# Top-k attention and max-out layers on one core: the GpSimd product of scores and signs in two halves, with a new order of work

## The chip, the cores and the metric

The kernel runs on one core of one Trainium2 chip. The metric is device time in microseconds (us) of one execution. The core has five engines with a queue each: TensorE (PE: matmuls, with their weight loads in a row of their own, PEld), VectorE (DVE), ScalarE (ACT), GpSimd (POOL) and SyncE (SP), which issues the transfers.

## What is computed

Attention with a top-k mask over 8 batches of 8 heads, 576 tokens, head size 64, and then a layer with the maximum of three products, for the 4608 tokens:

```python
def _attn_ref(q, k, v):
    top_k = 32
    scores = matmul(q, k.transpose(0, 1, 3, 2)) / sqrt(D)
    kth = np.partition(scores, -top_k, axis=-1)[..., -top_k:-top_k + 1]
    scores = np.where(scores >= kth, scores, -1000000000.0)
    attn = np.exp(scores - np.max(scores, axis=-1, keepdims=True))
    attn = attn / (np.sum(attn, axis=-1, keepdims=True) + 1e-09)
    return np.matmul(attn, v)

def _moe_ref(x, w1, w2, w3, w_out):
    h = np.maximum(np.maximum(x @ w1, x @ w2), x @ w3)
    return h @ w_out
```

d_model is 512, d_ff 768; everything is float32.

## The kernel before

**Attention** runs in 144 units. A unit is 128 query rows of a pair of heads (or the last 64 rows of two pairs), so it has two score tiles of 128 x 576. Its steps, with their keys in the order's table: scores on PE (`q`, L508) and their copy out of PSUM on ACT (`e`, L516); the top eight of each of 7 column groups on DVE (`s0`, `s1`, L525); from these a pivot close to the 32nd largest (`N` on POOL, L531; `p1` to `p5` on DVE, L539 to L557, of which `p4`, L554, reads two tiles of SBUF). Then for each of the two score tiles: the sign of score against pivot on ACT with a count (`g`, L564), the product of scores and signs on POOL (`w`, L569, function `window`), and the top eight of that product on DVE (`k`, L573, `below`), which gives the candidates next to the pivot. Small steps on POOL (`i`, `j`, L580 to L586) and DVE (`h`, L591) pick the 32nd largest. The mask on DVE (`m`, L614, a `scalar_tensor_tensor` that reads the scores twice) follows, then the exponential on ACT (`x`, L623), the denominator (POOL L629, DVE L633, ACT L638), transposes on PE (`T`, L664 to L669) with copies on ACT (`E`, L681), and for a group of units the product with v (`v`, L700), scaled on DVE (`y`, L710) and split into two float16 parts (`Y` on ACT L724, `Z` on POOL L728).

**Weights** come in at the start and are decoded on DVE (L254 to L260), scaled and cut into float16 halves (L272 to L334); `wi_scaled` is the list of the three steps that give the scales of w1, w2 and w3.

**The layers** (`mlp`) run for each batch in two or three pieces of its columns: 36 matmuls for each of six blocks of d_ff (L757), their maximum on ACT and DVE (L764, L766), two parts of h (ACT L769, POOL L772), the second layer (L817), a scaled copy (L822) and the store. A piece can start when the attention of its columns is done. The layers fill PE between attention's steps; the last batch's stand at the end.

**The order** of the instructions of every engine is made ahead by `in_order`: a greedy planner with a cost for each step, a rank (the unit's number plus an entry of `OFFSETS` by step) and waiting times between engines (`GAP`, `NEAR`, `LATE`). `SWITCH` is the price of changing PE's mode (scores use halves of its rows, the product with v halves of its columns); `STICK` says how much later a step may start to keep PE in such a mode; `PATIENCE` how much later than the earliest one a step of better rank may start; `LEAD` how far ranks may run ahead. Steps marked `alone` (p4, the masks, the decoding) are planned with POOL's queue in mind (`LOCK_A`, `LOCK_B`). The engines then run their queues in that order and wait for each other by semaphores.

Of the kernel before, what the change touches and what calls it, by code (L numbers as in the profile page):

```python
# [14 lines left out]
ALU = mybir.AluOpType  # L15
# [9 lines left out]
NSSB = 5  # L25
NWB = 6
PMB = 2
GAP = 67.0
NEAR = 182.0
SWITCH = 100.0  # L30
STICK = 204.0
WINDOW = 150
LEAD = 49.1
LOCK_A = -150.0
LOCK_B = -100.0
OFFSETS = {'E0': -2.08, 'E1': -11.9, 'E2': 1.81, 'N': -19.09, 'T0': 7.0, 'T1': 7.99, 'T2': 7.02, 'Y': -1.5, 'Z': -8.28, 'd':
# [9 lines left out]
RANK_M = -20.0  # L46
LATE = {'PE': 160.0, 'DVE': 85.0, 'ACT': 100.0, 'POOL': 40.0, 'SP': 2000.0}

# [1 line left out]
class Piece:  # L50
# [7 lines left out]
    def seen(self, engine):  # L58

        if engine == self.engine:  # L60
            return self.start + self.cost + (NEAR if engine in ("DVE", "ACT") else 0.0)
        return self.start + self.cost + LATE[self.engine] + GAP

# [6 lines left out]
def in_order(pieces, fill):  # L70
# [35 lines left out]
    while left:  # L106
        best = None
        low = min((q[0].rank for q in queues.values() if q), default=0.0)
        for e in LATE:
            some = [x for x in queues[e][:WINDOW] if x.rank <= low + LEAD]  # L110
            some = some + fills[e][:1] if e == "PE" else fills[e][:1] + some
            could = [(t, x) for x in some if (t := ready(x)) is not None]
            if could:
                first = min(t for t, _ in could)
                stays = [c for c in could if c[1].mode and c[0] <= first + STICK] if e == "PE" and mode[0] else []
                t, x = stays[0] if stays else next(c for c in could if c[0] <= first + PATIENCE[e])
                if best is None or t < best[0]:
# [13 lines left out]
        left -= 1  # L131


PATIENCE = {'PE': 162, 'DVE': 131, 'ACT': 0, 'POOL': 85, 'SP': 0}


@with_exitstack
def kernel(ctx, tc, q, k, v, moe_w1, moe_w2, moe_w3, moe_w_out, out):
    nc = tc.nc
    B, NP, _, S = q.shape  # L140
    D = v.shape[-1]
    P = 128
    C = S // 64
    NU = S // P
    DM, DF = moe_w1.shape
    DO = moe_w_out.shape[1]
    KC = DM // P
    FC = DF // P
    HALF = S // 2
# [61 lines left out]
    CUTS = {DF: DF // 2, DO: DO}  # L211
# [131 lines left out]
    def piece(engine, cost, run, needs=(), rank=0.0, takes=(), mode=None, alone=False, tag=""):  # L343
        x = Piece(engine, cost, run, needs, rank + OFFSETS.get(tag, 0.0), [(rings[r], rel) for r, rel in takes], mode, alone)
        pieces.append(x)
        return x
# [9 lines left out]
    lows = {}  # L356
# [47 lines left out]
    wo_scaled, wi_scaled = [], []  # L404
# [161 lines left out]
    def window(n, t):  # L566

        d = st[n]
        nc.gpsimd.tensor_tensor(d["w"][t], d["ssb"][t], d["w"][t], ALU.mult)  # L569

    def below(n, t):
        d = st[n]
# [161 lines left out]
    def mlp(b, first, spans, tiles, alone, needs, rank):  # L734
# [6 lines left out]
        def add(engine, cost, run, needs=(), takes=(), mode=None):  # L741
            x = Piece(engine, cost, run, needs, rank, [(rings[r], rel) for r, rel in takes], mode)
            every.append(x)
            if engine == "PE":
                if products:
                    x.needs.append(products[-1])
                products.append(x)
            return x

        def layer(i, f, kcs, c0, c1, box):  # L750
            xh, xl = x_of[b]
            if kcs[0] == 0:
                box["ps", i] = ps_m.tile([P, 512], F32, name="m")
            for kc in kcs:
                high, low = halves(i, kc, f * P, P)
                for k, (a, bb) in enumerate(((high, xh), (low, xh), (high, xl))):
                    nc.tensor.matmul(box["ps", i][:, :c1 - c0], a, bb[:, kc, c0:c1], start=(kc == 0 and k == 0),  # L757
                                     stop=(kc == KC - 1 and k == 2))

        def largest(i, w, box):  # L760
            ps, prev = box.pop(("ps", i)), box.get("h")
            h1 = box["h"] = wk.tile([P, WIDE], F32, name="h1", bufs=3)
            if i == 0:
                nc.scalar.activation(h1[:, :w], ps[:, :w], AF.Copy, scale=rises[:, 0:1])  # L764
            else:
                nc.vector.scalar_tensor_tensor(h1[:, :w], ps[:, :w], rises[:, i:i + 1], prev[:, :w], ALU.mult, ALU.max)  # L766

        def high_h(f, cs, w, box):
            nc.scalar.copy(H[0][:, f, cs], box["h"][:, :w])  # L769

        def low_h(f, cs, w, box):
            nc.gpsimd.tensor_tensor(H[1][:, f, cs], box["h"][:, :w], H[0][:, f, cs], ALU.subtract)  # L772

        for c0, c1 in spans:
            w = c1 - c0
            base = min(c0, 2 * P)
            cs = slice(off + c0 - base, off + c1 - base)
            for f in range(FC):
                box, prev, before = {}, None, []
                for i in range(3):  # L780
                    rel = []
                    for kcs in ((0, 1), (2, 3)):
                        x = add("PE", 6 * max(0.434 * w, 64.0), lambda i=i, f=f, kcs=kcs, c0=c0, c1=c1, box=box: layer(i, f, kcs, c0, c1, box),
                                [*needs, *(lows[i * KC + kc, f * P // CUTS[DF] * CUTS[DF]] for kc in range(KC) if lows)],
                                [("m", rel)] if kcs[0] == 0 else [])
                    now = []
                    y = add("DVE" if i else "ACT", 85 + 1.2 * w if i else 125 + 0.97 * w, lambda i=i, w=w, box=box: largest(i, w, box),
                            [x, *prev] if i else [x, *wi_scaled], [("h1", now)])
                    rel.append(y)
                    if i:  # L790
                        before.append(y)
                    before, prev = now, [y]
                y = add("ACT", 87 + 0.85 * w, lambda f=f, cs=cs, w=w, box=box: high_h(f, cs, w, box), prev)
                z = add("POOL", 2.7 * w, lambda f=f, cs=cs, w=w, box=box: low_h(f, cs, w, box), [y])
                before.extend([y, z])
                done.setdefault(f, []).append(z)
# [22 lines left out]
        def scaled_out(n, both, box):  # L819
            so = so_of["both", b] if both else so_of[b]  # L820
            box["ob"] = io.tile([P, DO], F32, name="ob")
            nc.scalar.activation(box["ob"][:n], box["po"][:n], AF.Copy, scale=so[:n])  # L822
# [11 lines left out]
        for u in tiles:  # L834
# [10 lines left out]
            y = add("ACT", 575, lambda n=n, both=both, box=box: scaled_out(n, both, box), [x, so_at[b]], [("ob", used)])  # L845
# [19 lines left out]
    def group_us(b, u):  # L865

        for g in ((0,), (1, 2), (3,)) if b == 0 else ((0, 1), (2, 3)):
            if u in g:
                return g
        return (u,)  # L870
# [14 lines left out]
    def attention(n):  # L885
# [34 lines left out]
        for t in range(2):  # L920
            p(("g", t), "ACT", 770, lambda t=t: sign(n, t), needs=[d["p5"], d["e"]])
            p(("w", t), "POOL", 1410, lambda t=t: window(n, t), needs=[d["g", t]])
            p(("k", t), "DVE", 668, lambda t=t: below(n, t), needs=[d["w", t]])
            held(n, "w", t).append(d["k", t])
# [121 lines left out]
    for b in range(B):  # L1046
        for first, spans, tiles in parts_of[b]:
            us = [u for u in range(NU + 1) if any(c0 < u * P + 64 <= c1 or c0 < (u + 1) * P <= c1 for c0, c1 in spans)]
            needs = [z for (hp, u), z in z_of[b].items() if set(group_us(b, u)) & set(us)]
            products, every, last = mlp(b, first, spans, tiles, False, needs, RANK_M)  # L1050
            fill.extend(every)
        x_done[b].append(last)
# [20 lines left out]
    with tc.If(redo != 0):  # L1073
        with tc.For_i(0, B, 1) as b:
# [6 lines left out]
            for hp in range(NP):  # L1081
# [5 lines left out]
                for u in (*range(NU), *((NU,) if hp % 2 else ())):  # L1087
                    i = len(units)
# [17 lines left out]
            for first, c0, c1, tiles in ((True, 0, 2 * P, (0, 1)), (False, 2 * P, S, range(2, NU + 1))):  # L1106
                for x in mlp(B, first, [(c0, c1)], tiles, True, [], 0.0)[1]:
                    x.run()
# [46 lines left out]
```

## Time and profile before

| | |
|---|---|
| median of 3 runs | 1251.83 us (1251.45 to 1253.36) |
| profiled execution | 1251.33 us, its span 1249.5 us |
| busy, PE / DVE / ACT / POOL | 93% / 91% / 83% / 69% of the span |
| mean granted TensorE clock | 0.976 of full speed |

Busy shares are over the whole span; the views by stretch tell more, since at the start the weights come in and at the end PE is alone. Matmuls are pipelined and their ends are modelled, so PE's busy time is a little more than its work. A line such as L569 is that of the kernel's text, an arrow in a row stands between what is written and what is read, and a bracket at the end of a timeline row holds the idle time before it and what ended it.

### The profile page before, as it was taken

The numbers are of one execution on the slowest core, as the hardware profiler recorded it, in microseconds if no ns is written. First come the engines' busy times: TensorE is split into PE (matmuls) and PEld (weight loads), VectorE is DVE, ScalarE is ACT, GpSimd is POOL, SyncE is SP. The second block draws the span as 40 slices with busy tenths as digits, with TensorE's granted clock in tenths as the row PEclk, the third lists the DMA queues.
The fourth block names the chain that finished last, engine by engine and source line by source line (L and its number), as shares of the span: only waits on it lengthen the run. The fifth ranks groups of instructions, "written<-read, shape, count | busy, mean of one in ns | idle before, by whom it ended". The sixth has DMA issues, their size and how long they took to land.

```text
span 1249.5 us, 30550 instructions
## 1 busy us (share of the span) xinstructions
PE 1158.7 (93%) x9891; PEld 839.8 (67%) x9891; DVE 1141.2 (91%) x5547; ACT 1036.4 (83%) x2406; POOL 866.0 (69%) x1293
## 2 busy tenths in 40 slices
PE   4677789998999999999999999999899999999997
PEld 2355568775776757676777768666676768776764
DVE  8999898999999999999999999999999999999511
ACT  3688899898789998899889998898888988998621
POOL 5456687876677787777787778767777777877410
PEclk9788899999899999999999999999899999999999
DMA  8440111100111011100111021101011010000000
GB/s 329 130 139 1 56 40 48 39 28 23 36 40 47 11 55 28 58 11 20 47 48 39 11 64 40 37 11 39 29 39 47 11 47 19 13 7 2 18 18 29
DMA packets 33864, 54.74 MB, mean 44 GB/s; under 512 B 12960, under 2 KB 12960, under 8 KB 33696
## 3 DMA queue, kind: packets, MB, share of 16 engines
q1 hardware_dynamic: 33696, 52.71, 13.5%
q8 instruction: 80, 1.31, 0.4%
q14 instruction: 88, 0.72, 0.2%
HBM read 43.25 MB, written 9.44 MB: 42 GB/s over the span
## 4 chain that ended last, share of the span: by engine, by line
PE 61%; DVE 27%; ACT 8%; issue 2%; POOL 1%; DMA 0%; ACTq 0%; DVEq 0%; POOLq 0%
PE m L757 26%; PE tr L700 9%; PE s L508 9%; PE tr L669 7%; DVE L L525 7%; PE m L817 6%; DVE ssb L614 5%; DVE Q L573 4%; ACT pm L623 2%; ACT w L564 2%; PE tr L664 2%; DVE h L766 1%; DVE z L554 1%; ACT ssb L516 1%; ACT pT L681 1%
## 5 line engine op out<-in xcount | busy, mean ns | idle before, releaser
L569 POOL TENSOR_TENSOR w<-ssb,w 128x576 f32<-128x576 f32 x288 | 432.0, 1506 | 62.0 <-ACT w L564 58.8
L757 PE MATMUL m<-xh,wall 128*128 128x256 f16 (+3 forms) x2448 | 438.4, 279 | 5.8 <-DVE h L766 3.2
L757 PEld LDWEIGHTS <-wall 128*128 128x128 f16 x3672 | 347.3, 98 | 82.5 <-issue 13.5
L757 PE MATMUL m<-xl,wall 128*128 128x256 f16 (+3 forms) x1224 | 339.0, 279 | 0.0
L525 DVE MAX8 L<-ssb 128x8 f32<-128x82 f32 (+1 forms) x2016 | 316.7, 228 | 2.2 <-ACT ssb L516 2.1
L623 ACT ACTIVATE pm<-ssb,nb 128x576 f32<-128x576 f32 x288 | 224.1, 780 | 49.6 <-DVE ssb L614 49.3
L614 DVE SCALAR_TENSOR_TENSOR ssb<-ssb,kth 128x576 f32<-128x576 f32 x288 | 257.6, 910 | 0.1
L681 ACT COPY pT<-tr 128x512 f32<-128x512 f32 (+1 forms) x432 | 217.7, 514 | 28.3 <-PE tr L666 17.9
L564 ACT ACTIVATE w<-ssb,Q 128x576 f32<-128x576 f32 x288 | 223.4, 778 | 15.7 <-DVE Q L557 14.1
L573 DVE MAX8 Q<-w 128x8 f32<-128x576 f32 x288 | 214.3, 748 | 3.7 <-POOL w L569 3.4
L669 PE MATMUL tr<-ident,pm 128*128 128x128 f32 x1152 | 179.7, 282 | 24.0 <-ACT pm L623 14.3
L508 PE MATMUL s<-kT,qT 64*128 64x288 f32 x1920 | 176.5, 320 | 19.2 <-ACT ssb L516 8.7
L700 PE MATMUL tr<-pT,vt 128*64 128x256 f32 (+2 forms) x2000 | 180.8, 331 | 2.2 <-ACT s L195 1.1
L508 PEld LDWEIGHTS s<-kT,qT 64*128 64x128 f32 x1920 | 139.6, 194 | 62.6 <-ACT ssb L516 22.5
L669 PEld LDWEIGHTS tr<-ident,pm 128*128 128x128 f32 x1152 | 131.1, 142 | 69.2 <-ACT pm L623 29.9
L516 ACT ACTIVATE ssb<-s 128x1152 f32<-128x1152 f32 x144 | 163.2, 1134 | 11.4 <-PE s L508 10.7
L700 PEld LDWEIGHTS tr<-pT,vt 128*64 128x64 f32 x2000 | 112.3, 140 | 63.1 <-issue 20.8
L766 DVE SCALAR_TENSOR_TENSOR h<-m,rises,h 128x256 f32<-128x256 f32 (+3 forms) x204 | 100.2, 491 | 53.6 <-PE m L757 51.4
L772 POOL TENSOR_TENSOR hl<-h,hh 128x256 f16<-128x256 f32 (+3 forms) x102 | 82.8, 811 | 74.8 <-ACT hh L769 73.1
L817 PE MATMUL m<-wall,hh 128*128 128x512 f16 x432 | 128.5, 379 | 0.1
L629 POOL TENSOR_SCALAR den<-sums 128x2 f32<-128x2 f32 x144 | 39.4, 273 | 83.1 <-ACT pm L623 73.5
L817 PE MATMUL m<-wall,hl 128*128 128x512 f16 x216 | 81.9, 379 | 0.0
(116 smaller groups left out, 1505.8 us busy)
## 6 DMA issues: line engine op xcount, KB each, us to landing
raw<-in_k_dram SPq DMA_DIRECT2D x36, 288.0 KB, 2.8
raw<-in_q_dram SPq DMA_DIRECT2D x36, 256.0 KB, 2.8
vt<-in_v_dram SPq DMA_DIRECT2D x32, 256.0 KB, 2.8
out_dram<-ob SPq DMA_DIRECT2D x32, 256.0 KB, 2.0
wall<-in_moe_w_dram SPq DMA_DIRECT2D x8, 768.0 KB, 6.5
wall<-in_moe_w_out_dram SPq DMA_DIRECT2D x3, 512.0 KB, 6.0
raw<-in_q_dram SPq DMA_DIRECT2D x36, 32.0 KB, 2.6
vt<-in_v_dram SPq DMA_DIRECT2D x64, 16.0 KB, 2.4
```

The costliest lines, as they stand in the source:

```text
L508: nc.tensor.matmul(s[:, h, i, :HALF], qT[sl, qa, c0:c0 + P], kT[sl, ka, i * HALF:(i + 1) * HALF], start=(n_ == 0 and a == 0), stop=(n_ == ...
L525: nc.vector.max(d["L"][:, t, g, :], d["ssb"][t][:, g * S // G:(g + 1) * S // G])
L564: nc.scalar.activation(d["w"][t], d["ssb"][t], AF.Sign, bias=d["Q"][:, t, 0:1], scale=-1.0, accum_out=d["cnt"][:, t:t + 1])
L569: nc.gpsimd.tensor_tensor(d["w"][t], d["ssb"][t], d["w"][t], ALU.mult)
L573: nc.vector.max(d["Q"][:, t, 1:NW], d["w"][t])
L614: nc.vector.scalar_tensor_tensor(ss, ss, d["kth"][:, t:t + 1], ss, ALU.is_lt, ALU.subtract, accum_out=d["lost"][:, t:t + 1])
L623: nc.scalar.activation(d["pm"][:, t], d["ssb"][t], AF.Exp, bias=d["nb"][:, t:t + 1], scale=-1.0 / SHRINK, accum_out=d["sums"][:, t:t + 1])
L669: nc.tensor.transpose(pt[:, j * P:(j + 1) * P], pm[:, i, 64 * i + j * P:64 * i + (j + 1) * P], ident)
L681: nc.scalar.copy(pT[:, 512 * i:512 * i + m] if i < 2 else pT[:, 8 * P:10 * P], pt[:, :m])
L700: nc.tensor.matmul(xp[64 * h:64 * h + 64, to], vt[:, 4 * h + i if i < 4 else 8 + h, :], keys, start=(i == 0), stop=(i == 4))
L757: nc.tensor.matmul(box["ps", i][:, :c1 - c0], a, bb[:, kc, c0:c1], start=(kc == 0 and k == 0), stop=(kc == KC - 1 and k == 2))
L817: nc.tensor.matmul(box["po"][:n], a[:, f, cs], bb, start=(f == 0 and k == 0), stop=(f == FC - 1 and k == 2))
```

## The change

In `window` the one product of 576 columns becomes two, of columns 0 to 287 and 288 to 575; what is computed is the same. The planner still sees one POOL step at the same cost. The layers' first products (`layer`) get one more need in the plan, the three weight scales. And the constants of the planner have other values, the 83 offsets among them.

```diff
-GAP = 67.0
-NEAR = 182.0
+GAP = 68.0
+NEAR = 181.0
-STICK = 204.0
+STICK = 72.0
-LEAD = 49.1
+LEAD = 47.8
-OFFSETS = {'E0': -2.08, 'E1': -11.9, 'E2': 1.81, 'N': -19.09, 'T0': 7.0, 'T1': 7.99, 'T2': 7.02, 'Y': -1.5, 'Z': -8.28, 'd':
+OFFSETS = {'E0': -2.38, 'E1': -11.42, 'E2': 2.15, 'N': -20.8, 'T0': 6.58, 'T1': 7.44, 'T2': 6.61, 'Y': -5.44, 'Z': -11.1, 'd':
...
-PATIENCE = {'PE': 162, 'DVE': 131, 'ACT': 0, 'POOL': 85, 'SP': 0}
+PATIENCE = {'PE': 114, 'DVE': 131, 'ACT': 29, 'POOL': 100, 'SP': 0}
...
     def window(n, t):
 
         d = st[n]
-        nc.gpsimd.tensor_tensor(d["w"][t], d["ssb"][t], d["w"][t], ALU.mult)
+        for c in (slice(0, HALF), slice(HALF, S)):
+            nc.gpsimd.tensor_tensor(d["w"][t][:, c], d["ssb"][t][:, c], d["w"][t][:, c], ALU.mult)
...
                         x = add("PE", 6 * max(0.434 * w, 64.0), lambda i=i, f=f, kcs=kcs, c0=c0, c1=c1, box=box: layer(i, f, kcs, c0, c1, box),
-                                [*needs, *(lows[i * KC + kc, f * P // CUTS[DF] * CUTS[DF]] for kc in range(KC) if lows)],
+                                [*needs, *wi_scaled, *(lows[i * KC + kc, f * P // CUTS[DF] * CUTS[DF]] for kc in range(KC) if lows)],
```

`HALF` is 288 and `S` 576.

## Rows read from the trace of the kernel before

**Rows 1.** The page, part 1: busy us, share of the span, instructions

```profile
PE 1158.7 (93%) x9891; PEld 839.8 (67%) x9891; DVE 1141.2 (91%) x5547; ACT 1036.4 (83%) x2406; POOL 866.0 (69%) x1293
```

**Rows 2.** Busy us by stretch: length, then engines (instructions), clock, DMA share, GB/s

```profile
0.00:187.00 187.00, 132.82 (x996) 89.98 (x998) 174.00 (x764) 142.24 (x316) 115.41 (x166) 0.89 0.34 116
187.00:900.00 713.00, 686.44 (x6052) 504.90 (x6049) 690.49 (x3448) 634.27 (x1487) 533.82 (x804) 0.99 0.12 35
900.00:1180.00 280.00, 277.20 (x2427) 203.19 (x2424) 265.31 (x1311) 247.52 (x581) 209.28 (x314) 1.00 0.08 23
1180.00:1250.00 70.00, 62.29 (x430) 41.78 (x428) 11.44 (x26) 12.40 (x24) 7.43 (x10) 0.98 0.06 21
```

**Rows 3.** The page, part 4: the chain that ended last, by engine

```profile
PE 61%; DVE 27%; ACT 8%; issue 2%; POOL 1%; DMA 0%; ACTq 0%; DVEq 0%; POOLq 0%
```

**Rows 4.** The masks: ns minimum/median/maximum; in the page, busy us and mean ns

```profile
L614 DVE SCALAR_TENSOR_TENSOR ssb<-ssb,kth x288: 789/810/2126, 35.3 to 1170.5; 128x576 f32<-128x576 f32 x144
...
L614 DVE SCALAR_TENSOR_TENSOR ssb<-ssb,kth 128x576 f32<-128x576 f32 x288 | 257.6, 910 | 0.1
```

**Rows 5.** POOL's products of 576 and of 18 columns, same columns as rows 4

```profile
L569 POOL TENSOR_TENSOR w<-ssb,w x288: 1395/1416/2057, 30.0 to 1166.0; 128x576 f32<-128x576 f32 x144
...
L569 POOL TENSOR_TENSOR w<-ssb,w 128x576 f32<-128x576 f32 x288 | 432.0, 1506 | 62.0 <-ACT w L564 58.8
...
L586 POOL TENSOR_TENSOR oh<-oh,Q x144: 212/226/834, 34.4 to 1169.2; 128x18 f32<-128x18 f32 x144
```

**Rows 6.** Timeline of POOL and DVE, 601 to 605 us: start us, us, instruction

```profile
601.74 1.42 POOL L569 TENSOR_TENSOR w<-ssb,w 128x576 f32<-128x576 f32 x1
601.74 2.03 DVE L614 SCALAR_TENSOR_TENSOR ssb<-ssb,kth 128x576 f32<-128x576 f32 x1
...
603.79 0.80 DVE L614 SCALAR_TENSOR_TENSOR ssb<-ssb,kth 128x576 f32<-128x576 f32 x1
```

**Rows 7.** Timeline of POOL and of DVE, 743 to 748 us

```profile
743.55 3.88 POOL L569 TENSOR_TENSOR w<-ssb,w 128x576 f32<-128x576 f32 x2
...
744.39 1.76 DVE L614 SCALAR_TENSOR_TENSOR ssb<-ssb,kth 128x576 f32<-128x576 f32 x1
```

**Rows 8.** DVE's timeline: the first and the last of 24 long ones

```profile
133.99 1.69 DVE L254 TENSOR_SCALAR ob<-xl 128x512 int32<-128x512 int32 x1
...
1154.35 1.68 DVE L614 SCALAR_TENSOR_TENSOR ssb<-ssb,kth 128x576 f32<-128x576 f32 x1
```

**Rows 9.** Busy us in four shorter stretches, columns as in rows 2

```profile
300.00:350.00 50.00, 42.17 (x357) 32.79 (x357) 46.07 (x229) 40.76 (x95) 35.68 (x56) 0.90 0.10 30
450.00:500.00 50.00, 45.79 (x421) 34.24 (x419) 48.90 (x232) 44.59 (x105) 38.71 (x59) 1.00 0.17 47
850.00:900.00 50.00, 45.37 (x350) 31.54 (x349) 47.34 (x239) 43.90 (x101) 36.05 (x55) 0.93 0.11 35
...
1050.00:1100.00 50.00, 49.33 (x469) 37.43 (x467) 49.34 (x250) 45.00 (x106) 41.56 (x59) 1.00 0.03 12
```

**Rows 10.** PE's timeline: two products with v, of the same size

```profile
286.14 2.38 PE L700 MATMUL tr<-pT,vt 128*64 128x256 f32 x20
...
318.60 4.22 PE L700 MATMUL tr<-pT,vt 128*64 128x256 f32 x20 [0.46 <-ACT pT L681]
```

**Rows 11.** Waits of DVE, 187 to 1180 us: us in total, times, longest

```profile
DVE Q L573 <- POOL w L569: 3.4, 8, 1.1
DVE kth L591 <- POOL oh L586: 2.5, 4, 1.3
DVE rs L633 <- POOL den L629: 1.3, 2, 0.9
```

18 rows, old and new, of the table OFFSETS are left out of this document.

## The prediction

> **What bounds the kernel now.** I read the busy shares of the page first, then the same by stretch, then the chain that ended last, and only then single lines. Over the whole span TensorE (PE) and VectorE (DVE) are both above nine tenths and GpSimd (POOL) is at 69% [rows 1]. By stretch [rows 2] the run has four parts. Up to 187 us PE is idle for 187 - 132.8 = 54 us while the weights are decoded and the first attention units run. From 187 to 900 us both are almost full: PE is idle for 713 - 686.4 = 26.6 us, DVE for 713 - 690.5 = 22.5 us. From 900 to 1180 us PE is idle for 2.8 us of 280 and sets the pace alone. After 1180 us only PE works, on the last batch's layers, which need that batch's attention. So the end is the work of PE plus the idle time that PE collects on the way, and nearly all of that idle time lies before 900 us. The chain agrees: PE has 61% of it, DVE 27%, POOL 1% [rows 3]. A gain on DVE is a gain of the run only where PE waits for attention: in the first 187 us and in thin stretches of the second part, of which 300 to 350 us is the worst [rows 9].
>
> The change touches one thing that DVE loses time to. The masks (L614) take 0.81 us in the median, 0.91 us in the mean, 2.13 us at most [rows 4]: most run undisturbed, and some are far longer. At 601.74 us one starts together with a product of L569 on POOL and takes 2.03 us; the next, with POOL at rest, takes 0.80 us [rows 6]. The long one ends its wait at 601.74 + 2.03 - 0.80 = 602.97 us, 0.19 us before the product ends at 603.16 us. So a two-input DVE instruction that starts while a product reads must let nearly the whole product pass. I went through DVE's timeline for all such cases (a two-input instruction, or a decode step of L254, that starts inside a product and is over 0.06 us longer than its form usually is): 53 of them, 35.9 us together. 24 of them waited over 0.8 us: 15 masks, 6 pivots of L554, 2 of the review (L646), 1 decode step; [rows 8] has the first and the last of the 24. They lie 3 before 187 us, 16 from 187 to 900 us, 5 after.
>
> **The change, part by part.** *Removed and added on POOL.* 288 products of 576 columns become 576 of 288. The trace has no product of 288 columns; between the two-input form of 18 columns (0.226 us) and that of 576 (1.416 us) [rows 5] a column costs (1.416 - 0.226) / 558 = 2.13 ns, so 288 columns take 0.226 + 270 x 2.13 ns = 0.80 us and the pair 1.60 us: 0.185 us more each, 288 x 0.185 = 53 us of POOL time. Bounds: none, if the second half's fixed part hid behind the first, and 65 us, if the whole 0.226 us came again. POOL has 1249.5 - 866 = 383 us idle [rows 1], so this lies beside other work. On the path it counts where a product is waited for: POOL's 1% of the chain is 12.5 us at most, and 13% longer products make that 1.6 us longer at most, 0 at least. I take 0.8 us. If that cover is gone, the price is that of the third rival.
>
> *What DVE gets back.* If DVE may start between the halves, a wait of over 0.8 us, which began in the first half, is 0.8 us shorter; one that began in the second half is as before. That is 24 x 0.8 = 19.2 us of DVE: 3 x 0.8 = 2.4 us before 187, 16 x 0.8 = 12.8 us from 187 to 900, 5 x 0.8 = 4.0 us after. In the last stretch PE is full, so I count nothing. In the others the bounds are none and all. In the second stretch DVE itself is idle for 22.5 us, which is time in which it waits for others and which more speed doesn't shorten, and with POOL busier a few new waits come; so I take half of each: 1.2 + 6.4 = 7.6 us. What is late next, where such a stall goes, is the exponential on ACT behind the mask, then the transposes on PE, and then PE's own queue.
>
> *Can DVE start between the halves?* At 743.55 us two products stand back to back and take 3.88 us, not 2 x 1.42; a mask that started at 744.39 us took 1.76 us [rows 7]. It waited for the first product, went before the second, and the second waited for it. So yes. The second half will then start up to 0.8 us late, which POOL's idle time hides. By the Trainium skill, "GPSIMD Engine Reference", section 2.1 (Instruction dispatch), consecutive GpSimd instructions aren't separated: each of its cores starts the next as soon as its own share is done. Taken alone, that would leave DVE no place between the halves: no gain, 0.8 us of price, 1252.1 us. The row at 743.55 us speaks against that, and the measurement decides, but it is one of the second rival's conditions.
>
> *The order.* The constants (offsets of the steps, STICK 204 to 72, PATIENCE of PE, ACT and POOL) change where each instruction stands in its queue on all five engines, the loads on SP among them; no instruction comes or goes by it. The new need of the layers on all three weight scales alters the plan of the first layers alone: they start at about 100 us, in the stretch that is idle anyway, and I count 0. What the order does can't be read from the trace of before. Its bounds are its worst stretches: one more like 300 to 350 us would cost 50 - 42.2 = 7.8 us of PE; closing that one, 450 to 500 and 850 to 900 would give 7.8 + 4.2 + 4.6 = 16.6 us [rows 9]. The clock goes with them: granted 0.90 on average in the first of the three, so part of it at the lower of its two levels (1.2 and 2.4 GHz), and a product with v takes 4.22 us there, behind idle time, against 2.38 us elsewhere [rows 10]. Nothing in the profile says which way it goes, and the 280 us after 900 leave an order no more than 2.8 us to win. I take 0.
>
> *Sum* against the profiled execution (1251.33 us: the span of 1249.5 and 1.8 around it): 1251.3 - 7.6 + 0.8 = 1244.5 us. The median of the three runs shown is 1251.83, 0.5 us above it, which is inside their spread.
>
> **The rivals.** *Everything lands* (B): the whole gain of DVE before 900 us shortens PE's idle time: 2.4 + 12.8 = 15.2 us, less 0.8: 1236.9 us. For it: PE's idle time there (54 and 26.6 us) is larger than the gain, and a stall that is closed gives clock back. Against: DVE's own idle time, and PE waits that no mask ends. A better order would land in the same place.
>
> *No change* (C): DVE gets no place between the halves, or it does and PE takes the whole gain as work left for later, so that the tail gets longer by what attention ends earlier. 1251.3 + 0.8 to 1.6, about 1252.5 us. For it: PE's 93%, its 61% of the chain, and the stretch after 900 us. Against: rows 7, and 26.6 us of idle time in the second stretch.
>
> *Slower, POOL becomes late* (D): POOL is an ordered queue, and its small steps (L531, L580 to L586, L629) stand behind the products; DVE waits for them. Its densest stretch, 1050 to 1100 us, has 41.6 us of 50 [rows 9]; with 53 / 1180 of 50 us = 2.2 us more that is 88%, before the second halves wait for DVE. Now DVE waits for POOL for only 3.4 + 2.5 + 1.3 = 7.2 us in 187 to 1180 us [rows 11]. If a fifth of the 53 us lands on the path, 10.6 us, the run is 1251.3 - 6.8 + 10.6 = 1255.1 us. The point from which it decides: when those waits of DVE grow by more than the 19.2 us that the halves give it, to over 26 us. Against: POOL's idle time is mostly waiting for ACT, so it is ahead of its inputs.
>
> **How the numbers follow.** Forecast (A) 0.45, its own range 1241 to 1248; B 0.18, 1236 to 1241; C 0.18, 1249 to 1254; D 0.19, 1254 to 1260. The likeliest is A: 1244.5 us. The range goes from B's price of whole cover, 1236, to a little over D's price, 1256, and leaves about 0.12 out. A difference of 0.2% (2.5 us) is about what a measurement of this kernel can tell from none. Faster by more: A and B, 0.63; within: C, 0.18; slower: D, 0.19.
>
> **What would show it.** L569 stands 576 times at about 0.80 us, POOL's busy time is 900 to 930 us. The mean of L614 falls from 0.91 to about 0.86 us, and no wait behind a product is over 0.8 us. DVE's busy time falls from 1141 to some 1122 us; PE's idle time from 187 to 900 us falls from 26.6 to about 20 us; the stretch in which only PE works stays at 70 us. If the DVE time falls and PE's idle time doesn't, C is right; if DVE's idle time behind L569, L586 and L629 goes over 26 us, D is. The prediction is wrong from the ground if L614 keeps its tail, or if PE's idle time changes by more than 10 us in a stretch where DVE's waits didn't change: then the order did it.

## The result and the profile after

The changed kernel takes 1221.04 us (median of 4 runs, 1217.77 to 1222.51) against 1252.59 us of the kernel before on the same chips. The ratio is 0.9744, with a 95% interval of 0.9721 to 0.9767: 31.5 us faster. The forecast was 1244.5 us in a range of 1236 to 1256. The sign was right, the size (6.8 us) was too small by a factor of more than four, and the time lies below the range.

The page of the changed kernel, part 1, answers to [rows 1]; its lines are one higher from L570 on.

```profile
PE 1152.6 (95%) x9891; PEld 835.8 (69%) x9891; DVE 1129.7 (93%) x5547; ACT 1034.7 (85%) x2406; POOL 916.5 (75%) x1581
```

POOL's busy time rose by 50 us where 53 were worked out, and DVE's fell by 11.5 us where 19 were. DVE's part can't make 31 us. The stretches, against [rows 2], say where it went: PE's idle time from 187 to 900 us fell from 26.6 to 713 - 708.7 = 4.3 us, DVE's from 22.5 to 13.2 us, and the stretch at the end starts some 28 us sooner.

```profile
0.00:187.00 187.00, 134.45 (x994) 90.08 (x995) 178.52 (x796) 147.00 (x329) 125.58 (x209) 0.89 0.36 118
187.00:900.00 713.00, 708.71 (x6373) 528.58 (x6371) 699.79 (x3557) 654.70 (x1536) 587.15 (x1022) 1.00 0.13 37
900.00:1150.00 250.00, 248.07 (x2080) 176.22 (x2079) 240.60 (x1171) 220.18 (x518) 196.23 (x342) 1.00 0.07 21
1150.00:1219.00 69.00, 61.40 (x449) 40.90 (x447) 10.82 (x25) 12.87 (x25) 7.55 (x11) 0.98 0.07 21
```

The three thin stretches of [rows 9] are closed, the last of them nearly, and with them the clock is back at 1.00, the upper of its two levels (2.4 GHz):

```profile
300.00:350.00 50.00, 49.96 (x479) 39.02 (x478) 49.57 (x250) 42.47 (x100) 42.19 (x70) 1.00 0.20 54
450.00:500.00 50.00, 50.00 (x481) 39.69 (x479) 48.95 (x247) 44.78 (x105) 41.40 (x73) 1.00 0.16 43
850.00:900.00 50.00, 48.53 (x477) 39.57 (x474) 49.17 (x248) 42.89 (x100) 41.41 (x75) 1.00 0.16 43
```

A half takes 0.798 us in the median (worked out: 0.80). The masks' mean fell from 0.910 to 0.893 us, and not to the 0.86 that the prediction named as a sign (to [rows 4, 5]; ns minimum/median/maximum, then busy us and mean ns):

```profile
L570 POOL TENSOR_TENSOR w<-ssb,w x576: 782/798/1458, 35.5 to 1137.9; 128x288 f32<-128x288 f32 x192
...
L615 DVE SCALAR_TENSOR_TENSOR ssb<-ssb,kth 128x576 f32<-128x576 f32 x288 | 253.7, 893 | 0.0
```

And DVE does get in between the two halves of one product. In POOL's and DVE's timelines a mask that starts 0.02 us behind the first half takes 1.40 us instead of 0.81, and the two halves take 2.08 us, where a pair takes 1.56 in the median of all 288: the second half waited for the mask.

```profile
959.20 2.08 POOL L570 TENSOR_TENSOR w<-ssb,w 128x288 f32<-128x288 f32 x2
...
959.21 1.40 DVE L615 SCALAR_TENSOR_TENSOR ssb<-ssb,kth 128x576 f32<-128x576 f32 x1
```

### The profile page after: what moved, and what is told of

Read it like the earlier page. It is cut to its first block, busy times and chain, and to the rows that moved or that the text cites. A ratio compares the mean times of both kernels' runs of the same rounds, so it can differ in the third digit from the quotient of the medians.

```text
span 1218.5 us, 30985 instructions
## 1 busy us (share of the span) xinstructions
PE 1152.6 (95%) x9891; PEld 835.8 (69%) x9891; DVE 1129.7 (93%) x5547; ACT 1034.7 (85%) x2406; POOL 916.5 (75%) x1581
## 5 line engine op out<-in xcount | busy, mean ns | idle before, releaser
L570 POOL TENSOR_TENSOR w<-ssb,w 128x288 f32<-128x288 f32 x576 | 472.2, 844 | 74.3 <-ACT w L564 71.9
L615 DVE SCALAR_TENSOR_TENSOR ssb<-ssb,kth 128x576 f32<-128x576 f32 x288 | 253.7, 893 | 0.0
L508 PE MATMUL s<-kT,qT 64*128 64x288 f32 x1920 | 173.2, 315 | 15.7 <-ACT ssb L516 8.5
L508 PEld LDWEIGHTS s<-kT,qT 64*128 64x128 f32 x1920 | 137.0, 191 | 60.8 <-ACT ssb L516 23.9
```

Source lines behind the costliest of these rows:

```text
L508: nc.tensor.matmul(s[:, h, i, :HALF], qT[sl, qa, c0:c0 + P], kT[sl, ka, i * HALF:(i + 1) * HALF], start=(n_ == 0 and a == 0), stop=(n_ == ...
L570: nc.gpsimd.tensor_tensor(d["w"][t][:, c], d["ssb"][t][:, c], d["w"][t][:, c], ALU.mult)
L615: nc.vector.scalar_tensor_tensor(ss, ss, d["kth"][:, t:t + 1], ss, ALU.is_lt, ALU.subtract, accum_out=d["lost"][:, t:t + 1])
```

## The experiments

Theory at the start: the halves are worth about the 7 us that the prediction gave them, and the new order, which it put at nothing, is worth the rest. Rivals: the halves carry nearly all; or neither is worth anything without the other.

**The two parts apart.** The halves in the old order (the two lines of `window` put into the kernel before; all queues but POOL's hold the same instructions in the same order as before):

```diff
-        nc.gpsimd.tensor_tensor(d["w"][t], d["ssb"][t], d["w"][t], ALU.mult)
+        for c in (slice(0, HALF), slice(HALF, S)):
+            nc.gpsimd.tensor_tensor(d["w"][t][:, c], d["ssb"][t][:, c], d["w"][t][:, c], ALU.mult)
```

> The halves alone, in the old order (old constants, no new need): every engine's queue as before but for the doubled products. If the halves carry the gain of 31 us, about 1225 us. If they are worth what the prediction gave them (7 us) and the new order does the rest, 1243 to 1247 us, with DVE's waits behind products about halved and PE's idle time between 187 and 900 us near 20 us instead of 26.6. If the new order is needed for the halves to be worth anything, 1250 us or more.

Measured: 1247.76 us, ratio 0.9956 (0.9944 to 0.9967), 5.5 us faster. The other two signs did not come: DVE's waits behind products fell from 35.9 to 26.0 us, not to half, and PE's idle time from 187 to 900 us is 713 - 686.9 = 26.2 us as before, not near 20:

```profile
187.00:900.00 713.00, 686.85 (x6023) 503.75 (x6022) 688.07 (x3447) 633.18 (x1487) 560.93 (x987) 0.99 0.12 35
```

The new order alone is the reverse of this edit in the changed kernel (in the traces PE, DVE and ACT run the same operations in the same order as in the changed kernel).

> The new order alone, each product in one piece of 576 columns. If the order carries the gain and the halves are worth some 7 us, 1226 to 1230 us. If the halves carry it, 1245 to 1252 us. If the order was fitted to the halves and suits nothing else, over 1245 us with long waits of DVE behind products (mean of the masks above 0.95 us).

Measured: 1229.52 us, ratio 0.9811 (0.9788 to 0.9835), 23.8 us faster. The two add up to 29.3 of 31.5 us. So for these two orders the first theory stands in its sizes: the order is worth three quarters, the halves about what they were said to be.

To see how, I drew up DVE's account up to the last mask. The end of the last mask is DVE's work, its waits behind POOL (inside its busy time; counted in the timeline as for the prediction, behind all POOL instructions) and its idle time. Behind it lies the tail in which almost only PE works. All in us, from each kernel's profiled execution; "idle for POOL" is the part of the idle time that the list of waits puts down to POOL. How work and waits part depends on what is taken as the usual length of a form, and is good to about 2 us:

```
kernel                         last mask   work  behind POOL  idle  (idle for POOL)  tail
before                           1171.3   1062.2     64.1     45.0        9.6        78.2
halves, old order                1168.4   1063.7     56.1     48.6       18.1        78.0
new order, whole products        1151.9   1061.5     60.5     29.9        4.1        75.4
changed kernel                   1143.4   1063.2     52.6     27.6        8.8        75.1
start's offsets alone            1150.3   1062.1     50.5     37.7        5.3        76.3
start's offsets and halves       1155.8   1064.6     51.0     40.2       14.0        76.7
changed kernel, three parts      1164.4   1066.5     51.9     45.9       27.3        74.8
before, less work on PE          1162.9   1057.4     69.5     36.0       12.3        62.3
before, less work on DVE         1165.6   1030.1     70.0     65.5       18.5        78.4
```

The first four rows hold the case. DVE's work is the same. The halves take some 8 us off the waits behind POOL, in either order; part of it comes back as idle time for POOL (8.5 us more in the old order, 4.7 in the new). The order takes 15 to 21 us off the idle time. In the old order the halves bring the last mask only 2.9 us forward and the span of the profiled execution is 3.1 us shorter, where the medians differ by 5.5: the account covers a good half of it. Waits of DVE for POOL with the halves in the old order (us in total, times, longest), where the kernel before has 3.4, 3.7 and 2.5 us up to its last mask ([rows 11] begins at 187 us):

```profile
DVE Q L574 <- POOL w L570: 10.1, 22, 1.2
DVE rs L634 <- POOL den L630: 4.5, 10, 1.7
DVE kth L592 <- POOL oh L587: 3.5, 8, 1.3
```

PE gives a second account, for its busy and its idle time make up the span (us, from the same executions):

```
kernel                       span   busy   idle to 187   187 to 900   after 900
before                     1249.5  1158.7         54.2         26.6        10.0
halves, old order          1246.4  1159.4         52.7         26.2         8.2
new order, whole products  1227.3  1151.0         54.1          9.8        12.5
changed kernel             1218.5  1152.6         52.6          4.3         9.1
```

The new order alone takes 16.8 us off PE's idle time between 187 and 900 us and nothing off the 54 us before; 2.5 us come back behind 900. Another 7.7 us are busy time: the same 9891 matmuls take less of it, while the mean granted clock goes from 0.976 to 0.986. The two products of [rows 10] show what a lower clock can cost (4.22 us at a granted clock of 0.55, 2.38 at 1.00); that it makes the whole of the 7.7 us is not shown by a run. Busy time of the new order with whole products, then its stretch from 187 to 900 us:

```profile
PE 1151.0 (94%) x9891; PEld 834.5 (68%) x9891; DVE 1135.9 (93%) x5547; ACT 1036.0 (84%) x2406; POOL 870.6 (71%) x1293
...
187.00:900.00 713.00, 703.21 (x6287) 522.89 (x6287) 696.95 (x3525) 649.51 (x1521) 550.51 (x822) 1.00 0.12 36
```

**Which constants.** The changed kernel with the old table, and the kernel before with the new table and the new need:

> The changed kernel with the old table OFFSETS; halves, the new need and the other new constants (STICK, PATIENCE, LEAD, GAP, NEAR) stay. If the scalar constants carry the order's part, 1222 to 1228 us; if the table does, 1240 us or more; if only the whole set fits together, slower than 1245 us.

Measured: 1238.2 us, ratio 0.9876 (0.9852 to 0.9901).

> The kernel before (one product of 576 columns) with the new table OFFSETS and the new need in the plan, the other constants old. If the table carries the order's part, 1226 to 1232 us; if the scalar constants do, 1245 to 1255 us; if only the whole set fits together, 1250 us or more.

Measured: 1241.11 us, ratio 0.9903 (0.9878 to 0.9927). Neither part of the constants alone reaches the 0.981 of the whole order, and the first of these ratios holds the halves as well. More they don't show: in the old order a change of GAP alone, below, gives 0.985 to 0.994, and both ratios lie inside that. (With the new constants and without the new need the planner finds no step that can start, and the need with the old constants was not run. The run with the start's offsets alone, below, has the order's whole gain without the need.)

Next the start. Up to the end of the first batch's last mask, the kernel before takes 204.2 us, with 15.7 us of DVE idle:

```profile
0.00:204.20 204.20, 150.02 (x1174) 103.21 (x1176) 188.55 (x840) 159.37 (x358) 125.72 (x186) 0.90 0.33 110
```

The new order with whole products takes 189.8 us, with 8.4 us idle. 24 instructions of DVE were moved behind that point, which is about 4 of the 14.4 us; 7 are idle time and 3 waits behind POOL:

```profile
0.00:189.80 189.80, 135.67 (x1074) 92.95 (x1074) 181.43 (x816) 152.42 (x343) 125.25 (x181) 0.93 0.36 117
```

So I exchanged the offsets of the weights' steps and first loads, 33 of the table's 75 entries, of which 32 differ (the text ahead of the prediction says 83; it is 75).

> The changed kernel with the old offsets of the weights' steps and of the first loads (33 of 75 entries). The new order ends the first batch's attention 14.5 us earlier. If the weights' places make that, it is lost: about 1233 us, DVE's idle time before the first batch's last mask back near 15 us from 9. If the offsets of the attention steps make it, 1219 to 1225 us. If orders are draws, 1226 to 1245 us with the loss anywhere.

Measured: 1242.85 us, ratio 0.9929 (0.991 to 0.9949). The first batch's last mask ends at 207.9 us, with 19.2 us of DVE idle, and most of the order's gain is lost.

> The complement: the kernel before with only the weights' and first loads' new offsets. If these make the 14.5 us at the start, 1236 to 1240 us with the first batch's attention ended near 190 us. If not, 1247 to 1256 us. If orders are draws, up to 1265 us.

Measured: 1228.32 us, ratio 0.9815 (0.9796 to 0.9834): the whole gain of the order. But not by the start: the first batch's last mask ends at 202.2 us.

The last mask of all comes 21 us sooner, and 19 of these are gained behind that point. Up to the last mask 13.6 us of waits behind POOL and 7.3 us of idle time are gone. My theory of the start fell with that. The new order's early start seems to need the weights' offsets together with the others, for neither of these two runs starts early; but an order can gain the same amount elsewhere.

**Is an order a draw?** I changed GAP, a waiting time of the planner, by 1 ns, after which most places of DVE's queue hold another instruction. Neighbours of the old order, with whole products:

> The kernel before with GAP 68 instead of 67: the control for the run above, on the other side. If orders are draws and the old one was searched for as well, slower than before: 1255 to 1270 us. If the old order was no better than its neighbours, 1245 to 1257 us. Either way the difference is the size that a change of order without any meaning has here.

> The kernel before with GAP 66 instead of 67, a second neighbour of the old order. If orders are draws around a mean of some 1244 us and the old order is a poor one, 1236 to 1250 us. If the neighbour with GAP 68 (ratio 0.9936) was the exception, 1251 to 1265 us.

> The kernel before with GAP 69: a third neighbour. Draws: 1236 to 1250 us. The old order as a good one: 1251 to 1265 us.

Measured, with GAP 68, 66 and 69: ratios 0.9936 (0.9917 to 0.9956), 0.9894 (0.9869 to 0.9919) and 0.9854 (0.9834 to 0.9874); 1243.68, 1240.28 and 1235.91 us. All three are faster than the kernel before, by 8 to 18 us. Neighbours of the new order, with halves:

> The changed kernel with GAP 67 instead of 68, a constant of the planner that by itself means nothing (a waiting time longer or shorter by 1 ns), but about 750 of DVE's 3043 queue entries then stand elsewhere. If the gain of the order comes from one setting that makes sense by itself, 1219 to 1224 us as the changed kernel. If the order is one good draw that all constants together were searched for, a neighbour loses part of it: 1226 to 1240 us, with DVE's idle time up to the last mask at 33 to 42 us instead of 27.6.

> The changed kernel with GAP 69: its second neighbour (GAP 67 gave 1226.9). If the new order is a good draw that neighbours don't reach, 1222 to 1240 us. If the new constants are better as a region, 1219 to 1224 us.

Measured, with GAP 67 and 69: 0.9804 (0.9784 to 0.9823) and 0.9763 (0.9743 to 0.9782); 1226.85 and 1224.41 us. The first is slower than the changed kernel's 0.9744, with DVE idle for 31.7 us up to the last mask; the second is not clear of noise. And their partners with whole products:

> The new constants with GAP 67 and whole products: the partner of the run with GAP 67 and halves (ratio 0.9804), a fifth pair. If the halves' gain is the fall in lock waits less the rise of DVE's waits for GpSimd, and the new region of orders has much POOL idle time where it counts, the whole products are slower: 0.983 to 0.990. If the region is fitted to the halves' lengths, over 0.990. If halves are worth nothing here, 0.978 to 0.983.

> The new constants with GAP 69 and whole products: the partner of the run with GAP 69 and halves (ratio 0.9763), a sixth pair. If halves gain wherever the order was searched for with them: 0.980 to 0.986. If worth nothing here: 0.974 to 0.979.

Measured: 0.981 (0.9789 to 0.9831) and 0.9819 (0.9802 to 0.9835). With the new order's 0.9811 that makes three orders of the new constants with whole products, all at 0.981 to 0.982, against 1.000 and 0.985 to 0.994 for four of the old. So one thing is shown: the old order was the worst of its neighbourhood, by 1.05% against the mean of the three others (0.9895), and a part of the order's 1.9% is no merit of the new constants. A second is likely: the new constants' orders are better by another 0.8% than that mean. All three lie below all four of the old, but the closest intervals touch (0.9854 and 0.9819), and three orders on each side are few. In all six kernels with the new constants (three orders, with halves and without) the first batch's last mask ended at 189.8 to 192.7 us; in the old orders, with halves or without, at 204.2 to 206.0 us.

**The halves in other orders.** With GAP 68 in the kernel before:

> The order of GAP 68 (ratio 0.9936 with whole products) with halves: a fourth order in which the halves are added. The first three gave -0.4%, -0.7% and +0.3%. What the halves bring is the fall of DVE's waits behind products less the rise of its idle time behind GpSimd. With 55 us of lock waits against 64 in the order of before there is less to win here: ratio 0.990 to 0.996. If the halves always help, 0.987 or less; if only in an order fitted with them, 0.997 or more.

Measured: 1244.91 us, ratio 0.993 (0.9909 to 0.9952), against 0.9936 with whole products: no difference.

> The kernel before with the new offsets of the weights' steps and first loads, and the halves: a third order in which the halves are added to an order that was not searched for with them (that order with whole products: ratio 0.9815 to before). If the halves are worth 5 to 9 us in any order, ratio 0.974 to 0.978, 1219 to 1224 us. If they need an order with many collisions, as that of before, and this one has few, 0.980 to 0.984.

Measured: 1232.76 us, ratio 0.9848 (0.9812 to 0.9883), against 0.9815 (0.9796 to 0.9834): slower if anything, though the intervals just overlap. The account points to why: here the waits behind POOL were down to 50.5 us already and don't fall (51.0), while the idle time for POOL grows from 5.3 to 14.0 us. The list of DVE's waits for POOL in the run with halves (lines are nine lower here):

```profile
DVE Q L565 <- POOL w L561: 4.7, 12, 0.7
DVE rs L625 <- POOL den L621: 4.7, 16, 0.5
DVE kth L583 <- POOL oh L578: 4.4, 9, 1.6
```

The six pairs (old; new; GAP 68 of old; GAP 67 and 69 of new; start's offsets) give -0.4, -0.7, -0.1, -0.1, -0.6 and +0.3%, a quarter of a percent or 3 us in the mean. The first, second and fifth are gains clear of noise; the other three can't be told from none.

Then more of the same dose, three parts instead of two:

```diff
-        for c in (slice(0, HALF), slice(HALF, S)):
+        for c in [slice(j * S // 3, (j + 1) * S // 3) for j in range(3)]:
```

> The changed kernel with each product in three parts of 192 columns. A part takes 0.226 + 174 x 2.13 ns = 0.60 us, the three 1.79 us against 1.60: GpSimd gets 55 us more. If shorter parts keep giving, DVE's waits behind products fall from 31 to about 20 us and the time to 1212 to 1218 us. If more collisions and the longer GpSimd queue eat it, 1219 to 1228 us, with DVE's idle time behind GpSimd growing.

Measured: 1242.11 us, ratio 0.9919 (0.9896 to 0.9942), 21 us slower than with halves. A part takes 0.593 us, as worked out. The waits behind POOL hardly fall (52.6 to 51.9 us), and DVE's idle time for POOL goes from 8.8 to 27.3 us. Both expectations were too low. DVE's waits for POOL, in the changed kernel:

```profile
DVE Q L574 <- POOL w L570: 4.0, 12, 0.8
DVE kth L592 <- POOL oh L587: 2.7, 6, 0.8
DVE rs L634 <- POOL den L630: 1.9, 7, 0.5
```

and with three parts:

```profile
DVE Q L574 <- POOL w L570: 13.8, 37, 1.0
DVE rs L634 <- POOL den L630: 8.9, 24, 0.9
DVE kth L592 <- POOL oh L587: 4.4, 12, 0.8
```

This is the prediction's third rival, near its point: it said that POOL becomes late when these waits go over 26 us. In its window, 187 to 1180 us, they are 25.1 us with three parts, against 7.2 before, 14.6 with the halves in the old order and 7.7 in the changed kernel. So POOL decides at three parts, not at two.

**Which engine sets the end?** In the kernel before, in its own order, I took work from one engine and then from the other.

```diff
-                for k, (a, bb) in enumerate(((high, xh), (low, xh), (high, xl))):
+                for k, (a, bb) in enumerate(((high, xh), (low, xh))):
```

> The kernel before in its own order, with the third of each three float16 products of the first layers left out (1224 of 3672 matmuls of L757, about 150 us of TensorE's work; the layers' output loses its low part). Ten orders so far agree with: span = 1063 us of DVE's work up to the last mask + DVE's waits behind GpSimd + DVE's idle time + a tail of about 75 us. If DVE's queue sets the end, only the tail gets shorter, by a third of its 44 us of L757, and DVE's idle time behind PE by up to 10 us: 1225 to 1236 us. If PE sets the pace from 187 us on, as the prediction had it, the end follows PE's work: under 1210 us.

Measured: 1222.79 us, ratio 0.9772 (0.9727 to 0.9817). Busy times up to the last mask and behind it:

```profile
0.00:1162.90 1162.90, 1000.59 (x8270) 687.02 (x8272) 1126.91 (x5510) 1014.03 (x2371) 853.02 (x1278) 0.97 0.15 46
1162.90:1250.00 87.10, 54.54 (x401) 35.86 (x397) 14.77 (x38) 16.34 (x36) 9.64 (x15) 0.97 0.05 17
```

PE has 104 us less to do (150 were expected), and the last mask comes 8.4 us sooner. The tail is 15.9 us shorter. That is 24 us in this profiled execution, the slowest of the three runs; by the medians it is 30.

```diff
             ps, prev = box.pop(("ps", i)), box.get("h")
+            if i == 2:
+                return
```

> The kernel before in its own order, with the maximum over the third of the layers' three products left out on DVE (102 of 204 instructions of L766, 50 us of DVE's work; the layers' output is that of two products). If DVE's queue sets the end, the last mask comes some 40 us earlier, until PE's work with its idle time at the start (1158.7 + 54 + 8 = 1220 us) stops it: 1215 to 1228 us. If PE sets the pace, DVE only gets more idle time: 1242 to 1250 us.

Measured: 1246.4 us, ratio 0.9958 (0.9942 to 0.9973).

```profile
0.00:1165.60 1165.60, 1083.46 (x9362) 788.61 (x9364) 1100.08 (x5419) 1017.16 (x2371) 856.48 (x1278) 0.98 0.15 46
1165.60:1250.00 84.40, 70.89 (x533) 48.56 (x529) 9.12 (x29) 16.56 (x36) 9.66 (x15) 0.97 0.05 17
```

32 us of DVE's work before the last mask are gone, 91 instructions fewer, and that mask comes 5.7 us sooner: idle time grew by 20.5 us, 8.9 of it idle time for POOL, and waits behind POOL by 5.9. PE's idle time up to the last mask stayed as it was (83.4 and 82.1 us). So neither engine's queue alone sets the pace. In a fixed order both are nearly full, and an engine that gets faster mostly waits longer for the others. What goes with a shorter time is an order in which both wait less: from the kernel before to the changed one PE's idle time up to the last mask fell from 83.4 to 58.8 us and DVE's from 45.0 to 27.6 us, together.

## Why the prediction was wrong

**The order: the step that failed.** "I take 0", within -16.6 and +7.8, and it was -23.8 us (22.2 between the profiled executions). The value had no reason but that the profile doesn't say which way an order goes, and the bound was too tight as well. It was PE's idle time in three thin stretches, with PE's work taken as fixed ("the end is the work of PE plus the idle time that PE collects on the way"). Between 187 and 900 us that idle time fell by 16.8 us with the order alone, as much as the bound; but PE's busy time fell too, by 7.7 us. The prediction had seen the other part of it ("The clock goes with them") and put no price on it. The 54 us of PE's idle time before 187 us, which looked like the room, stayed. On DVE's side the prediction counted nothing for the order, though 64 us of waits behind POOL and 45 us of idle time lay before the last mask; with the order alone the idle time fell by 15.1 us and the waits by 3.6, and with the start's offsets alone the waits by 13.6.

**The halves: right in sum, by luck.** Forecast -6.8 us, measured -5.5 in the old order. A half's length and DVE's entry between halves came out as worked out; POOL's busy time rose by 45 us in the old order (866.0 to 910.7), where 53 were worked out. But of the 19.2 us that DVE should get back, in the old order only 9.9 us came: its waits behind products fell from 35.9 to 26.0 us. They became shorter (none over 0.66 us behind a half in the changed kernel) and more: 53 before, 80 with the halves, since twice the instructions and a longer POOL queue are met more often. The prediction named those new waits and gave them no number. The price on the path, taken at 0.8 us within 0 to 1.6, was 8.5 us of idle time for POOL, 6.7 of them behind the product itself (L569 of before, 3.4 to 10.1 us) and 1.8 behind the small steps (L629 and L586 of before). POOL's 1% of the chain did not bound it. And the 6.4 us that should come out of PE's idle time between 187 and 900 us did not come there: it fell by 0.4 us. So the sum is near because its errors cancelled in this order; over six orders the halves gave from -8.5 to +4 us.

**What bounds the kernel.** "PE sets the pace alone from 900 us" is half of it. With 104 us less on PE the end came 24 us sooner in the profiled execution, 16 of these in the tail; with 32 us less on DVE 5.5 us. The two are coupled by the order.

**The rivals.** *Everything lands* (1236.9 us) was the nearest, and its remark that a better order would land in the same place was the point to build on. Its own condition, that DVE's gain before 900 us all shortens PE's idle time, did not hold: with the halves in the old order that idle time fell by 1.9 us. *POOL becomes late* didn't decide at two parts and did at three. *No change* by a missing entry between the halves didn't happen; the Trainium skill's rule about cores that go on without each other ("GPSIMD Engine Reference", section 2.1) doesn't keep DVE out, as the rows at 959.20 us show.

**What stays open.** Why the old order fell at the bad end of its neighbours, and which of the thousands of moved instructions make the new constants' orders better behind the start. How much of the order's gain is the clock is not separated either. The six kernels with the new constants agree on the earlier start, but one order gained as much without it.

## What to carry to other kernels

Where a kernel's queues are ordered by a search, a change that comes with a new search must be judged with two controls: the change in the old order, and neighbours of the old order; here a meaningless change of one constant moved the time by 0 to 1.5%, the halves by 0 to 0.7%. Bound what an order can win by all waits and idle time of the nearly full engines and by what a higher granted clock would take off TensorE's busy time, not by the worst stretches; that is a loose bound (109 us of waits and idle time on DVE here, of which the order won 19). Cutting instructions to free a shared resource is a dose: count the waits that get shorter, the new ones, and what waits for the longer queue, for two parts gained 0.7% in the new order, and three lost 1.8% against them.

## What the hardware showed that I had not expected

A wait of DVE behind a POOL product ends before the product does, by 0.19 us for whole products ([rows 6]: 602.97 against 603.16 us) and likewise for halves: at 959.21 us a mask goes on after 1.40 - 0.81 = 0.59 us, at 959.80, and the half it waited for ends at 960.00. In all 33 masks of the changed kernel that waited over 0.2 us for one half alone the difference is 0.19 to 0.20 us, and with three parts too. That piece doesn't shrink with the length of the product.

Two instructions on POOL, 288 columns each, cost 2 x 0.798 - 1.416 = 0.18 us more than one; three of 192 cost 3 x 0.593 - 1.416 = 0.36 us more. The fixed part is 0.18 us each time. Back to back the records overlap a little: a pair takes 1.56 us from start to end and three parts 1.70 in the median, so 0.14 us remain of each 0.18.
